# A second Strassen level for three of the seven products of the first GEMM, in a kernel of retention and a two-layer network

## The chip, the cores and the metric

The kernel runs on one core of one Trainium2 chip. The metric is the time of one execution on the device, in microseconds (us); lower is better. A core has a matrix engine (TensorE, PE in the profile), a vector engine (VectorE, DVE), a scalar engine (ScalarE, ACT), a general engine (GpSimd, POOL), and a queue that issues most transfers (SyncE, SP). Each runs its own instructions in the order in which they were written, and waits on semaphores where it needs another's result.

## The reference

A retention layer feeds a two-layer network. 4 batches, 8 heads, 768 steps, head size 64; the result is seen as 3072 tokens of 512 features; the network has 2048 hidden features. All is float32.

```python
for t in range(S):
    state = gamma[None, :, None, None] * state + np.einsum('bhd,bhe->bhde', k[:, :, t], v[:, :, t])
    y[:, :, t] = scale * np.einsum('bhd,bhde->bhe', q[:, :, t], state)
x = np.ascontiguousarray(attn_out.transpose(0, 2, 1, 3)).reshape(B * S, H * D)
h = x @ w_in
g = np.where(h > 0.0, h, alpha * (np.exp(np.minimum(h, 0.0)) - 1.0))
return (g @ w_out).astype(np.float32)
```

## The kernel before, in words

The tokens are cut into six blocks of 512, counted from 1 here (tb 0 to 5 in the code). For each block the kernel runs GEMM 1 (hidden = input times w_in), the ELU, and GEMM 2 (output = hidden times w_out). Data lie transposed: features on partitions, tokens along the free dimension. The retention of the next block (scores, states, outputs; L257 to L350) is put between pieces of GEMM 2, and writes the next block's input into xb.

Block 1 is multiplied plainly. From block 2 on, both GEMMs use the Winograd form of Strassen's algorithm (strassen, L455): each matrix is cut into four quarters, and seven products of quarters, summed up in a certain way, take the place of eight. Products 1, 6 and 5 are added up in one PSUM bank (pa) one after the other, with a copy to SBUF by ScalarE after each (kept, L447), products 7 and 4 in a second (pd), product 2 in a third (pb). VectorE adds a bank and a kept copy (plus, L452). The left factors are sums of weight quarters, made once (combine_w_in for w_in, combine_w_out for w_out); the right factors are differences of quarters of the input (combine_x into xt for GEMM 1).

GEMM 1 is run in four parts n, one for each four of the sixteen tiles of 128 hidden rows: two tiles of the upper half and the two of the lower half that belong to them. A part with its four results C11, C12, C21, C22 (two row tiles by 256 tokens each) is called a quadruple here. Each product of a part is four matmuls of 128x128 weights and 256 columns (L497), so one of the seven products takes 16 matmuls in a block. Each result goes through the ELU (elu, L370): relu and exp on ScalarE into a tile r, and later one operation on VectorE that puts max(h, exp - 1) into the hidden tiles gC11 to gC22. That last operation is kept in a list, later, and written into VectorE's order when the next ELU starts. When a part's C12 is done, two differences are made, T3 = C22 - C12 and T1 = C12 - C11 (L509), T1 in the place of C12.

GEMM 2 of block 2 has one level (second), with combine_w_out beside it, which also stores second-level weights to scratch2. From block 3 on GEMM 2 has two levels (second_twice): each of its seven products is itself made of seven, of four matmuls with 128 columns each (L618). The right factors of a product are four differences (inputs, L607) into a tile ts, of which there are two; the weights come from DRAM, 256 KB each, through a ring of 11 tiles (fetch_small): each use of a tile is followed by the fetch of the one 11 further on, in the order of the list USE. The ring lies in memory that the pools stage and t4 used before, and opens when GEMM 2 of block 2 is over.

The order on each engine is that of the program text, since it asks for a manual schedule. The main loop (L784) lets the parts of GEMM 1 overlap: it starts products 1 and 2 of a part before products 3 and 4 of the part before (the generator tail), and does the same between GEMM 1 and GEMM 2 and between blocks. The next block's q, k and v are loaded on SP in GEMM 1 (load), and v is scaled on GpSimd as it lands (scale_v, L239).

## Time and profile before

The median of 8 runs is 663.36 us (661.96 to 665.23). The profile is of one execution.

| | before |
|---|---|
| profiled execution | 665.23 us |
| its span, first to last instruction | 663.2 us |
| mean granted TensorE clock | 0.994 |
| TensorE busy | 641.1 us (97%) |
| VectorE busy | 434.8 us (66%) |
| ScalarE busy | 228.9 us (35%) |
| GpSimd busy | 24.4 us (4%) |
| blocks 3, 4, 5, 6 start on TensorE at | 252.58, 354.31, 457.55, 563.14 us |
| moved by DMA | 123.64 MB, 186 GB/s |

Busy time is the time in which an engine has an instruction at work, a weight load (PEld) being counted apart. A group in the profile is all instructions of one source line, engine and operation; what stands behind "idle before" is how long the engine stood before them and what ended it. The chain is found from the last instruction backwards. "issue" is time in which an engine waited for nothing that the profile shows.

### The profile page before, as it was taken

What the parts mean: (1) busy time and instruction counts of PE and PEld (TensorE: products, weight loads), DVE (VectorE), ACT (ScalarE), POOL (GpSimd) and SP (SyncE); (2) the same over time, 40 slices, a digit from 0 to 9 for tenths busy, and PEclk for the clock granted to TensorE, in tenths of its full rate; (3) what the DMA queues carried; (4) which work ended last, traced back from release to release, by engine and by line L of the source; (5) the groups of instructions that cost most, each with busy time, mean ns of one, the idle gap of its engine ahead of it and who ended that gap; (6) DMA issues with size and microseconds to landing.
All of it is one profiled execution on the core that took longest, in us unless ns stands there. A gap on an engine that the chain in (4) does not pass through costs nothing.

```text
span 663.2 us, 14662 instructions
## 1 busy us (share of the span) xinstructions
PE 641.1 (97%) x6144; PEld 540.8 (82%) x6144; DVE 434.8 (66%) x769; ACT 228.9 (35%) x432; POOL 24.4 (4%) x28
## 2 busy tenths in 40 slices
PE   4899999999999999999999999999999899999997
PEld 4764455458888888889999889899889899888996
DVE  5698678566757744549765557767357948355974
ACT  7477542014541002543112553112455111455211
POOL 1000100001100000200000200000200000000000
PEclk9899999999999999999999999999999989999999
DMA  9648977549115758505777604677702758300793
GB/s 341 233 145 302 333 232 234 144 134 374 71 64 167 249 207 278 230 1 189 218 217 235 240 1 123 213 229 247 289 0 62 246 165 266 109 1 16 220 305 128
DMA packets 63825, 123.64 MB, mean 186 GB/s; under 512 B 5136, under 2 KB 22544, under 8 KB 61712
## 3 DMA queue, kind: packets, MB, share of 16 engines
q1 hardware_dynamic: 63760, 122.70, 55.7%
q8 instruction: 49, 0.80, 0.5%
q14 instruction: 16, 0.13, 0.1%
HBM read 100.66 MB, written 22.02 MB: 185 GB/s over the span
## 4 chain that ended last, share of the span: by engine, by line
PE 95%; DVE 2%; DMA 1%; issue 1%; SPq 0%; ACT 0%; DVEq 0%
PE pa L497 21%; PE pa L618 15%; PE pd L497 10%; PE pd L618 7%; PE hp L396 6%; PE pb L497 5%; PE pa L410 4%; PE pa L555 4%; PE pb L618 4%; PE pd L555 2%; PE kv L287 2%; PE y L335 2%; PE pd L410 2%; PE pb L410 2%; PE y L311 2%; PE sc L265 2%
## 5 line engine op out<-in xcount | busy, mean ns | idle before, releaser
L452 DVE TENSOR_TENSOR h<-pd,m 128x512 f32<-128x512 f32 x42 | 29.1, 692 | 86.5 <-ACT m L447 69.5
L447 ACT COPY m<-pa 128x512 f32<-128x512 f32 x63 | 36.4, 578 | 109.6 <-PE pa L497 73.7
L626 ACT COPY ms<-pa 128x128 f32<-128x128 f32 x84 | 22.4, 266 | 127.6 <-PE pa L618 124.5
L374 ACT ACTIVATE r<-r 128x512 f32<-128x512 f32 x96 | 60.7, 632 | 3.0
L618 PE MATMUL pd<-ts,wq 128*128 128x128 f32 x448 | 59.9, 277 | 0.3 <-DVE res L630 0.3
L618 PE MATMUL pa<-ts,wq 128*128 128x128 f32 x448 | 59.2, 275 | 0.0
L373 ACT ACTIVATE r<-h 128x512 f32<-128x512 f32 x60 | 38.0, 632 | 57.1 <-DVE h L452 57.1
L618 PEld LDWEIGHTS pd<-ts,wq 128*128 128x128 f32 x448 | 54.5, 192 | 1.2 <-DVE res L630 0.9
L618 PEld LDWEIGHTS pa<-ts,wq 128*128 128x128 f32 x448 | 54.8, 192 | 0.2
L618 PE MATMUL pa<-gC,wq 128*128 128x128 f32 x384 | 52.1, 278 | 0.4 <-ACT ms L626 0.4
L376 DVE SCALAR_TENSOR_TENSOR gC<-r,h 128x512 f32<-128x512 f32 x60 | 42.0, 700 | 11.4 <-ACT r L374 11.4
L618 PEld LDWEIGHTS pa<-gC,wq 128*128 128x128 f32 x384 | 47.3, 192 | 1.7 <-ACT ms L626 0.5
L239 POOL TENSOR_TENSOR kvn<-kvn,vf 128x512 f32<-128x512 f32 x20 | 22.4, 1119 | 456.1 <-DMA kvn<-in_qkv_dram 397.0
L497 PE MATMUL pa<-xb,w_s 128*128 128x256 f32 x160 | 37.8, 379 | 0.0
L497 PE MATMUL pa<-xb,w_a 128*128 128x256 f32 x160 | 37.8, 379 | 0.0
L497 PE MATMUL pa<-xt,w_s 128*128 128x256 f32 x160 | 37.8, 379 | 0.0
L497 PE MATMUL pa<-xt,w_b 128*128 128x256 f32 x160 | 37.8, 379 | 0.0
L497 PE MATMUL pd<-xt,w_b 128*128 128x256 f32 x160 | 37.8, 379 | 0.0
L497 PE MATMUL pb<-xb,w_a 128*128 128x256 f32 x160 | 37.8, 379 | 0.0
L497 PE MATMUL pd<-xt,w_s 128*128 128x256 f32 x160 | 37.8, 379 | 0.0
L630 DVE TENSOR_TENSOR res<-pd,ms 128x128 f32<-128x128 f32 x56 | 16.1, 288 | 29.1 <-PE pd L618 26.7
L497 PEld LDWEIGHTS pa<-xt,w_b 128*128 128x128 f32 x160 | 30.4, 190 | 4.1
(121 smaller groups left out, 1100.6 us busy)
## 6 DMA issues: line engine op xcount, KB each, us to landing
wq<-scratch_dram SPq DMA_DIRECT2D x196, 256.0 KB, 4.0
wraw<-in_w_dram SPq DMA_DIRECT2D x16, 1024.0 KB, 6.0
qk<-in_qkv_dram SPq DMA_DIRECT2D x24, 512.0 KB, 8.7
kvn<-in_qkv_dram SPq DMA_DIRECT2D x24, 512.0 KB, 9.3
scratch_dram<-so SPq DMA_DIRECT2D x22, 512.0 KB, 3.3
ws<-scratch_dram SPq DMA_DIRECT2D x7, 1024.0 KB, 7.1
scratch_dram<-w_s SPq DMA_DIRECT2D x8, 512.0 KB, 7.4
out_dram<-res SPq DMA_DIRECT2D x12, 256.0 KB, 3.3
```

Source lines behind the costliest of these rows:

```text
L239: eng.tensor_tensor(out=kv[:, 1], in0=kv[:, 1], in1=vf[:, i].unsqueeze(2).to_broadcast([C, H, D]), op=ALU.mult)
L373: nc.scalar.activation(r, h, AF.Relu, scale=-1.0)
L374: nc.scalar.activation(r, r, AF.Exp, scale=-1.0)
L376: later.append(lambda: nc.vector.scalar_tensor_tensor(g, r, -1.0, h, ALU.add, ALU.max))
L396: nc.tensor.matmul(hp, lhsT=w[n][:, fi, j // 2, j % 2, :], rhs=xb[:, j, :], start=(j == 0), stop=(j == 3))
L410: nc.tensor.matmul(ops[d], lhsT=wo[:, row, d * P : (d + 1) * P], rhs=g_plain[row * NF + f], start=(f == 0 and row == 0), stop=(f == NF - 1 ...
L447: nc.scalar.copy(m, ps)
L452: nc.vector.tensor_tensor(out=h, in0=ps, in1=m, op=ALU.add)
L497: nc.tensor.matmul(ps[:, fi, :], lhsT=w[:, fi, j2, :], rhs=x[:, j2, :], start=(begin and fi == 0 and j2 == 0), stop=(j2 == 1), skip_group_ ...
L555: nc.tensor.matmul(ps[:, d, :], lhsT=ws[:, 2 * d + f // 4, f % 4, :], rhs=gq[INPUT2[j]][:, f, :], start=(begin and f == 0 and d == 0), sto ...
L618: nc.tensor.matmul(ps, lhsT=w[:, f, :], rhs=ts[j][k][:, f, :], start=(begin and f == 0), stop=(f == 3), skip_group_check=True,)
L626: nc.scalar.copy(m, ps)
```

## The change

From the third block on (tb 2 to 5), three of GEMM 1's seven products, M2, M3 and M7, are each made by seven smaller ones (first_twice), over all 2048 hidden rows at once: four matmuls of 128 columns for each. Their second-level weights (four of seven; the rest are quarters of the weights as they are) are summed up on GpSimd in block 2 (combine_small), stored to a new scratch3, and fetched through the same ring, which now opens with the last product of block 2's GEMM 2 (change); their right factors are made by combine_x_twice. The finished M2, M3, M7 are put into gC11, gC12 and gC22, where the hidden values will be.

After that the quadruples are worked one by one: M1, M6 and M5 are added up in a bank of their own (first_rest into qa), M4 in pd, and five sums on VectorE end in the results (first_end and sixth): C11 = M1 + M2, u2 = M1 + M6 + M7, C22 = M1 + M6 + M5 + M7, C12 = M1 + M6 + M5 + M3, C21 = u2 + M4. ScalarE makes no copies here. elu gets a depth: the last operation of an ELU is put behind up to two later ones, and r has three tiles. T3 is made behind C12's ELU; T1 is now made in GEMM 2, as C22 - C11 after C11 has become T3 + C11 (later_t1). The loads of the next block are issued between the products of first_twice, its scalings written between the quadruples. combine_x runs at the start of a block. In block 2, combine_w_in runs two steps at a time and earlier, and the first fetches of w_out come after GEMM 1. GEMM 2 and the retention are the same matmuls as before.

```diff
-    w_a = [const.tile([P, 2, 2, 2, P], FP32, name=f"w_a{n}") for n in range(NQ)]
-    w_b = [const.tile([P, 2, 2, 2, P], FP32, name=f"w_b{n}") for n in range(NQ)]
-    w_s = [const.tile([P, 3, 2, 2, P], FP32, name=f"w_s{n}") for n in range(NQ)]
+    w_a_, w_b_ = (const.tile([P, NQ, 2, 2, 2, P], FP32, name=x) for x in ("w_a", "w_b"))
+    w_s_ = const.tile([P, NQ, 3, 2, 2, P], FP32, name="w_s")
+    w_a, w_b, w_s = ([x[:, n] for n in range(NQ)] for x in (w_a_, w_b_, w_s_))
...
-    def elu(g, h):
-        r = epool.tile([P, 512], FP32, name="r", tag="r")
-        nc.scalar.activation(r, h, AF.Relu, scale=-1.0)
-        nc.scalar.activation(r, r, AF.Exp, scale=-1.0)
-        flush()
-        later.append(lambda: nc.vector.scalar_tensor_tensor(g, r, -1.0, h, ALU.add, ALU.max))
+    def elu(g, h, depth=1, then=None):
+        r = epool.tile([P, 512], FP32, name="r", tag="r", bufs=3)
+        e = r if len(h.shape) == 2 else r.rearrange("p (a c) -> p a c", c=P)
+        nc.scalar.activation(e, h, AF.Relu, scale=-1.0)
+        nc.scalar.activation(e, e, AF.Exp, scale=-1.0)
+        def last():
+            nc.vector.scalar_tensor_tensor(g, e, -1.0, h, ALU.add, ALU.max)
+            if then:
+                then()
+        while len(later) >= depth:
+            later.pop(0)()
+        later.append(last)
...
+            if j == 4:
+                behind_last()
...
+    TWICE = [2, 3, 7]
+    SMALL = {5: 0, 6: 1, 7: 2, 3: 3}
+    small_w, to_fetch, before = [], [], []
+    for tb in range(2, NTB):
+        for j in TWICE:
+            m1, m2, *mine = [(tb, 0, j, k) for k in (1, 2, 6, 7, 5, 4, 3)]
+            to_fetch += [m1] + before[:1] + [m2] + mine[:2] + before[1:] + mine[2:3]
+            before = mine[3:]
+        to_fetch, before = to_fetch + before, []
+        for j in ORDER2:
+            mine = [(tb, 1, j, k) for k in (1, 2, 6, 7, 5, 3, 4)]
+            to_fetch += mine[:2] + before + mine[2:5]
+            before = mine[5:]
+        to_fetch, before = to_fetch + before, []
+    to_fetch = [x for x in to_fetch if x[1] == 1 or x[3] in SMALL]
     def fetch_small():
         if not to_fetch:
             return
-        tb, j, k = to_fetch.pop(0)
+        name = to_fetch.pop(0)
+        _, which, j, k = name
         t = ring.tile([P, 4, P], FP32, name="wq", tag="wq")
-        if k in (1, 2, 4):
+        if k in SMALL:
+            n = SMALL[k]
+            nc.sync.dma_start(
+                t.rearrange("p f d -> p (f d)"), (scratch3, scratch2)[which][j - 1, :, 512 * n : 512 * n + 512]
+            )
+        else:
             q = 4 * SLOT[j] + {1: 0, 2: 1, 4: 3}[k]
             nc.sync.dma_start(t.rearrange("p f d -> p (f d)"), scratch[q])
+        small_w.append((name, t))
+    W_IN = {2: w_a_[:, :, :, 1], 7: w_s_[:, :, 1], 3: w_s_[:, :, 2]}
+    def combine_small(j):
+        t = stage.tile([P, 4, 4, P], FP32, name="wi", tag="stage")
+        a11, a12, a21, a22 = (W_IN[j][:, 2 * r : 2 * r + 2, :, c, :] for r in range(2) for c in range(2))
+        s1, s2, s3, s4 = (t[:, k].rearrange("p (n f) c -> p n f c", f=2) for k in range(4))
+        tt = lambda o, x, y, op: nc.gpsimd.tensor_tensor(out=o, in0=x, in1=y, op=op)
+        tt(s1, a21, a22, ALU.add)
+        tt(s2, s1, a11, ALU.subtract)
+        tt(s3, a11, a21, ALU.subtract)
+        tt(s4, a12, s2, ALU.subtract)
+        nc.sync.dma_start(scratch3[j - 1], t.rearrange("p k f d -> p (k f d)"))
+    xs = {}
+    def quarters_of_input(t, b11, b12, b21, b22):
+        sub = lambda o, x, y: nc.vector.tensor_tensor(out=o, in0=x, in1=y, op=ALU.subtract)
+        sub(t[:, 0], b12, b11)
+        yield
+        sub(t[:, 1], b22, t[:, 0])
+        yield
+        sub(t[:, 2], b22, b12)
+        yield
+        sub(t[:, 3], b21, t[:, 1])
+    def combine_x_twice(part):
+        if part == 0:
+            xs[0] = tpool.tile([P, 4, 4, P], FP32, name="ts", tag="ts")
+            b = [xb[:, 2 + k].rearrange("p (h t c) -> p t h c", h=2, t=2)[:, u] for k in range(2) for u in range(2)]
+            names, at = (2, 3), slice(0, 2)
         else:
...
+            b = [xt_[:, 2:3, k, P * u : P * u + P] for k in range(2) for u in range(2)]
+            names, at = (7,), slice(2, 3)
+        t = xs[0][:, :, at]
+        for _ in quarters_of_input(t, *b):
+            pass
+        for n, j in enumerate(names):
+            b11, b12, b21, b22 = (x[:, n] for x in b)
+            xs[j] = {1: b11, 2: b21, 3: b22, 4: t[:, 3, n], 5: t[:, 0, n], 6: t[:, 1, n], 7: t[:, 2, n]}
+    PLACE = {2: "C11", 3: "C12", 7: "C22"}
+    def first_twice(tb, j):
+        dst = PLACE[j]
+        place = lambda name, r, t: gq[name][:, 4 * r : 4 * r + 4, P * t : P * t + P]
+        full = lambda t: t.rearrange("p a (b c) -> p (a b) c", c=P)
+        def product(k, ps, begin):
+            if k in SMALL:
+                name, w = small_w.pop(0)
+                assert name == (tb, 0, j, k)
+                lhs = [w[:, f, :] for f in range(4)]
+            else:
+                r, c = {1: (0, 0), 2: (0, 1), 4: (1, 1)}[k]
+                lhs = [W_IN[j][:, 2 * r + f // 2, f % 2, c, :] for f in range(4)]
+            for f in range(4):
+                nc.tensor.matmul(
+                    ps[:, f, :], lhsT=lhs[f], rhs=xs[j][k], start=(begin and f == 0), stop=True,
+                    skip_group_check=True,
+                )
+            if k in SMALL:
+                fetch_small()
+        def lift(ps, o=None):
+            if o is None:
+                o = full(mpool.tile([P, 2, TH], FP32, name="m", tag="m"))
+            nc.scalar.copy(o, ps)
+            return o
+        def plus(r, t, ps, m):
+            nc.vector.tensor_tensor(out=place(dst, r, t), in0=ps, in1=m, op=ALU.add)
+        pa = full(bank("a"))
+        product(1, pa, True)
+        m1 = lift(pa)
+        yield
+        pb = full(bank("b"))
+        product(2, pb, True)
+        plus(0, 0, pb, m1)
+        product(6, pa, False)
+        u2 = lift(pa)
+        pd = full(bank("d"))
+        product(7, pd, True)
+        m7 = lift(pd)
+        yield
+        product(5, pa, False)
+        plus(1, 1, pa, m7)
+        yield
+        product(4, pd, False)
+        plus(1, 0, pd, u2)
+        yield
+        product(3, pa, False)
+        lift(pa, place(dst, 0, 1))
+    def first_rest(n, j, ps):
+        w, x = {
+            1: (w_a[n][:, :, 0], xb[:, 0:2, half[0]]), 6: (w_s[n][:, 0], xt[1]), 5: (w_b[n][:, :, 0], xt[0]),
+            4: (w_b[n][:, :, 1], xt[3]),
+        }[j]
+        for fi in range(2):
+            for j2 in range(2):
+                nc.tensor.matmul(
+                    ps[:, fi, :], lhsT=w[:, fi, j2, :], rhs=x[:, j2, :],
+                    start=(j in (1, 4) and fi == 0 and j2 == 0), stop=(j2 == 1), skip_group_check=True,
+                )
+    def first_end(n, name, ps, x=None):
+        g = gq[name][:, 2 * n : 2 * n + 2, :]
+        nc.vector.tensor_tensor(out=g, in0=ps, in1=g if x is None else x, op=ALU.add)
+        g = g.rearrange("p a b -> p (a b)")
+        def combine():
+            mine = lambda x: gq[x][:, 2 * n : 2 * n + 2, :].rearrange("p a b -> p (a b)")
+            nc.vector.tensor_tensor(out=mine("T3"), in0=mine("C22"), in1=mine("C12"), op=ALU.subtract)
+        return lambda: elu(g, g, 2, combine if name == "C12" else None)
+    def later_t1(ns):
+        for n in ns:
+            mine = lambda x: gq[x][:, 2 * n : 2 * n + 2, :].rearrange("p a b -> p (a b)")
+            nc.vector.tensor_tensor(out=mine("T1"), in0=mine("C22"), in1=mine("C11"), op=ALU.subtract)
...
             if j == 2:
+                flush()
                 next_input(2)
             if j == 5:
                 next_input(6)
...
+                if j == 6:
+                    later_t1((0, 1))
                 next(cur)
+                if j == 6:
+                    later_t1((2, 3))
...
-    for j in ORDER2[:3]:
-        fetch(1, j)
+    ring = tpool = None
...
+    sides = itertools.chain(combine_w_in(1), combine_w_in(2)), combine_w_in(3), iter(()), iter(())
+    smalls = [2], [], [7], [3]
+    for n in range(NQ):
+        load(2 * CPB + n)
+        cur = first(n)
+        for at in range(3):
+            next(cur)
+        for _ in tail:
+            pass
+        for s in cur:
+            next(sides[n], None)
+            next(sides[n], None)
+            if s == "gap":
+                break
+        for _ in sides[n]:
+            pass
+        tail = cur
+        for j in smalls[n]:
+            combine_small(j)
+    for j in ORDER2[:3]:
+        fetch(1, j)
+    for m in range(2 * CPB, 3 * CPB):
+        scale_v(m)
+    def change():
+        nonlocal ring, tpool
+        early.close()
+        ring = ctx.enter_context(tc.tile_pool(name="ring", bufs=RING))
+        tpool = ctx.enter_context(tc.tile_pool(name="tpool", bufs=2))
+        for _ in range(RING):
+            fetch_small()
+        combine_x_twice(0)
+    cur = second(1, change)
+    next(cur)
+    next(cur)
+    for _ in tail:
+        pass
+    flush()
+    for step, s in enumerate(cur):
+        retention_step(2, step)
+    tail = iter(())
+    for tb in range(2, NTB):
         more = tb + 1 < NTB
...
+        qa = []
+        def rest(n, j):
+            if j == 1:
+                qa.append(ps_r.tile([P, 2, TH], FP32, name="qa", tag="r"))
+            first_rest(n, j, qa[n])
+        rest(0, 1)
+        for _ in tail:
+            pass
+        combine_x()
+        combine_x_twice(1)
+        rest(1, 1)
+        tail = iter(())
+        for at, j in enumerate(TWICE):
+            cur = first_twice(tb, j)
             next(cur)
+            next(tail, None)
             next(cur)
             for _ in tail:
                 pass
...
+            if at == 2:
+                first_end(1, "C11", qa[1])()
             next(cur)
...
+            if at == 1:
+                first_end(0, "C11", qa[0])()
             tail = cur
+            if more:
+                load((tb + 1) * CPB + at)
+        next(tail)
+        next(tail, None)
+        if more:
+            load((tb + 1) * CPB + 3)
+        u2 = {}
+        def sixth(n):
+            rest(n, 6)
+            u2[n] = mpool.tile([P, 2, TH], FP32, name="m", tag="m")
+            nc.vector.tensor_tensor(out=u2[n], in0=qa[n], in1=gq["C22"][:, 2 * n : 2 * n + 2, :], op=ALU.add)
+        def fourth(n):
+            pd = bank("d")
+            first_rest(n, 4, pd)
+            return first_end(n, "C21", pd, u2[n])
+        sixth(0)
+        for n in range(NQ):
+            if n < 2:
+                rest(n + 2, 1)
+                first_end(n + 2, "C11", qa[n + 2])()
+            elif n == 2:
+                fourth(1)()
+            else:
+                fourth(2)()
+            rest(n, 5)
+            ends = [first_end(n, name, qa[n]) for name in ("C22", "C12")]
+            ends[0]()
+            if n < 3:
+                ends[1]()
+            if n == 0:
+                fourth(0)()
+            if n < 3:
+                sixth(n + 1)
+            if n == 1:
+                sec = second_twice(tb, (lambda: combine_x_twice(0)) if more else lambda: None)
+            if more:
+                scale_v((tb + 1) * CPB + n)
+            if n in (1, 2):
+                next(sec)
+        next(sec)
+        ends[1]()
+        end = fourth(3)
+        next(sec)
+        end()
+        flush()
+        for step, s in enumerate(sec):
+            if step > 0:
+                retention_step(tb + 1, step - 1)
+            if s == ORDER2[-1]:
+                break
+        tail = sec
```

## The prediction

> **What bounds the kernel now.** I read the page's busy table and its chain first, then the groups, the waits of TensorE, and at last the timeline of one block, engine by engine.
>
> ```profile
> PE 641.1 (97%) x6144; PEld 540.8 (82%) x6144; DVE 434.8 (66%) x769; ACT 228.9 (35%) x432; POOL 24.4 (4%) x28
> ...
> PE 95%; DVE 2%; DMA 1%; issue 1%; SPq 0%; ACT 0%; DVEq 0%
> ```
>
> TensorE is busy for 97% of the span and is 95% of the chain. VectorE has a third of its time free, on average over stages. The waits of TensorE from 252 us on name little:
>
> ```profile
> PE kv L287 <- issue: 2.2, 1, 2.2
> PE sc L265 <- issue: 2.1, 2, 1.3
> PE y L311 <- issue: 0.5, 1, 0.5
> PE pa L618 <- ACT ms L626: 0.4, 1, 0.4
> PE pd L618 <- DVE res L630: 0.3, 2, 0.2
> ```
>
> So nearly every wait for another engine is hidden, and each matmul removed is worth its pitch, until one of these waits comes out. TensorE's timeline gives the pitches (start, duration, group; the record counts a float32 matmul twice):
>
> ```profile
> 357.76 1.05 PE L618 MATMUL pa<-gC,wq 128*128 128x128 f32 x8
> 358.65 1.06 PE L618 MATMUL pd<-ts,wq 128*128 128x128 f32 x8
> 359.55 1.89 PE L497 MATMUL pa<-xt,w_s 128*128 128x256 f32 x8
> 361.28 1.89 PE L497 MATMUL pd<-xt,w_s 128*128 128x256 f32 x8
> 363.00 1.89 PE L497 MATMUL pa<-xt,w_b 128*128 128x256 f32 x8
> ```
>
> Starts are 1.727 us apart for four matmuls of 256 columns, 0.893 us for four of 128. Durations overlap and are no price. VectorE's timeline, in the same way:
>
> ```profile
> 365.55 0.69 DVE L452 TENSOR_TENSOR h<-pd,m 128x512 f32<-128x512 f32 x1 [4.63 <-ACT m L447]
> 366.16 0.68 DVE L376 SCALAR_TENSOR_TENSOR gC<-r,h 128x512 f32<-128x512 f32 x1
> ...
> 370.49 1.08 DVE L376 SCALAR_TENSOR_TENSOR gC<-r,h 128x512 f32<-128x512 f32 x1 [0.76 <-ACT r L374]
> 371.84 0.69 DVE L452 TENSOR_TENSOR h<-pd,m 128x512 f32<-128x512 f32 x1 [0.26 <-PE pd L497]
> 372.44 0.68 DVE L376 SCALAR_TENSOR_TENSOR gC<-r,pa 128x512 f32<-128x512 f32 x1
> 373.16 1.20 DVE L509 TENSOR_TENSOR gT<-gC,gC 128x512 f32<-128x512 f32 x1
> ```
>
> A 512-column operation takes 0.69 us, the next follows 0.61 us after its start, or 0.72 us if it reads the result (372.44 to 373.16). VectorE starts 0.20 us after TensorE's next group (371.84 after 371.64), ScalarE likewise. The two long ones, 1.08 and 1.20, lie beside GpSimd's operations, which began at 369.99 and 372.77 and take 1.04 us.
>
> **What the Trainium skill says.** "VectorE: DVE Perf Modes", section on the TRN2 errata, gives (N+151)/0.96 ns for a float32 tensor_tensor: 691 ns for 512. The trace has 692. "SBUF — State Buffer", section "Who interferes with whom": a DVE instruction with two SBUF inputs contends with a GpSimd one that reads SBUF, one with a single SBUF input doesn't. The trace agrees: both long operations read two SBUF tiles, and the PSUM sum at 371.84 is not longer. "TensorE: Matmul & The Clock Gate", section "Back-to-back issue gap": spacing is not proportional to columns, short matmuls pay more per column. Here 0.893 against half of 1.727, which is 0.864.
>
> **The change part by part.** I number the GEMM's seven Winograd products M1 to M7 and the seven inside one of them p1 to p7; blocks count from 1, so blocks 3 to 6 change.
>
> *TensorE.* M2, M3 and M7 took 16 matmuls of 256 columns each, 4 x 1.727 = 6.91 us. They become 28 of 128 columns, 7 x 0.893 = 6.25 us. That saves 0.66 us a product, 1.96 a block, 7.8 us in four blocks. M1, M4, M5, M6 keep 64 matmuls in the block in another order; GEMM 2 and the retention keep theirs.
>
> *VectorE.* A quadruple (two row tiles of the hidden layer) had three sums from PSUM, four ELU ends, two differences: 9 operations. It now has five sums, four ends, T3, and T1 later: 11. The three split products add nine sums a block, their inputs eight short operations. That is 8 + 9 long ones (10.4 us) and about 2.5 us, on some 66 us busy in a block of 102 us: still below TensorE's total. What decides is where they lie; I laid the listed orders of the three engines beside each other with the prices above. Four places don't close.
>
> (1) Before p6 of M7. p6 adds on the bank of p1, so it waits for ScalarE's copy m1, which is queued behind the ELU of C11 of quadruple 0, whose VectorE sum is queued behind M3's sum after p5. From the start of M3's p5: 0.89 + 0.20, the sum ahead 0.61, the C11 sum 0.72, relu 0.67, exp 0.54 to the next (pitches 366.27, 366.94, 367.48 on ScalarE), copy 0.58, 0.04 to TensorE: 4.25 us. TensorE has four groups of 0.893 in between, 3.57 us. It stands 0.68 us, and 0.1 us more for the restart (after the wait at 657.06 the next group came 0.1 us late).
>
> (2) In the quadruples. From the end of M1 of quadruple 3 to u2 of quadruple 3, VectorE has 18 operations in order, C11 to u2, two or three of them dependent: 18 x 0.61 + 3 x 0.12 = 11.3 us, and 0.12 to the consumer. The M5 of quadruple 3 waits for that u2; TensorE has seven groups from the start of that M1, 12.09 us, less 1.93 until VectorE can start: 10.16 us. Shortfall 1.26 us, with restart 1.35.
>
> (3) Next, p7 of GEMM 2's first product wants bank d, freed by the C21 sum of quadruple 3: ten operations, a short one and the last latency, 7.15 us, against 6.86 us: 0.3 us.
>
> (4) After the states of the retention. Four T1 differences, 2.44 us, now stand ahead of the seven state updates (0.48 us apart at 323.16). From the end of GEMM 2's p4 of product 2 to p4's sum of product 6: 0.29 + 5 x 0.61 + 0.16 + 2.44 + 0.21 + 7 x 0.46 + 0.60, about 10.0 us with latencies, against eight groups and the states, 8 x 0.893 + 2.15 = 9.3 us. TensorE's p7 of product 7 waits 0.7, with restart 0.8. Block 6 has no retention.
>
> GpSimd's four scalings a block move: the loads are issued about 10, 16, 22 and 25 us into the block on SP, behind small-weight fetches that wait for TensorE, and land 9 us later; two scalings then fall into the quadruples. Each lengthens an ELU end, T3 or input difference by 0.4 to 0.5 us, or nothing beside a PSUM sum. I take 0.5 in all, ends 0 and 1.5.
>
> Sum for blocks 3 to 5: 0.8 + 1.35 + 0.3 + 0.8 + 0.5 = 3.75, less 1.96: +1.8 each, 5.4 us. Block 6: 0.8 + 1.35 + 0.3 - 1.96 = +0.5.
>
> *Block 2.* combine_w_in comes two at a time, eight operations of 0.61 to 0.72 in quadruple 0, beside nine others in 12.1 us: VectorE has the time, but a sum may come late. GpSimd gets 12 operations[...] for the small weights; they lie under TensorE and cost only by slowing VectorE. Three stores of 1 MB and the ws loads behind them on SP: an estimate from the trace: the last combined weights are there at about 170 us, eight GpSimd operations take 9 us, a store 3.3 us, so the last is stored at 182; the first ws lands 7.1 us after its issue and is wanted at 191.5. I take 0.5 us, ends 0 and 3.
>
> *DMA.* 48 more fetches of 256 KB, landing in 4.0 us. The ring of 11 is issued 11 products ahead, 9.8 us at 0.893. In block 3 the first can't start before M4 of GEMM 2 frees its staging tile (252.58), and p6 of M2 comes 2 x 1.727 + 2 x 0.893 = 5.2 us later; 0.4 + 4.0 fits by 0.8. Zero taken, up to 4 us once. Renamed weight tiles, the third r buffer and the T1 formula cost nothing of their own: no engine issues more for them. The tail is as before.
>
> *Total.* The waits put down to "issue", 4.9 us, lie in retention bursts; some may vanish where TensorE has stood shortly before. I take 0.6 off. 5.4 + 0.5 + 0.5 - 0.6 = +5.8 us on the profiled execution, span 663.2, execution 665.23. That one is the slowest of the eight shown; I add the change to the median, 663.36: **669.2 us**. Under 0.2% (1.3 us) a measurement of this kernel can't tell from no change.
>
> **Rivals.** *VectorE keeps up*, the other side: all four places close and the matmuls' 7.8 us come off: 655.5. For it: VectorE's total is below TensorE's. Against it: the quadruples need 18 operations in 10.16 us, 0.56 us each, and no row is that fast. It gets faster as soon as the new waits are below 1.96 us a block. *Even*: half of the waits are real, and they stand in for the "issue" waits: 8 of new waits against 7.8: 663.5. *Worse*: GpSimd's scalings fall where VectorE is late (1.0 more in three blocks), block 3's ring is late by 3, block 2 gives up 2: 669.2 + 8 = 677. *The matmuls don't get shorter*, as 128-column ones with weights from w_a were not seen: their weight loads are 128x128 in both rows, so I hold this below 2 in 100; it adds to Worse.
>
> **How the numbers follow.** Forecast (666 to 673): 0.61. Worse (673 to 678): 0.15. Even (662 to 665): 0.12. Faster (654 to 661.5): 0.12. Leaving out the lower tail and half of Worse gives 661 to 675. Faster 0.13, the same 0.10, slower 0.77.
>
> **What would show it.** Right: TensorE's page row near 6432 instructions, the busy total of VectorE some 45 us up; TensorE's waits name ScalarE's m copy four times at 0.7, u2 on VectorE at 1 us or more, res and gC21 sums. Wrong: VectorE idle in the quadruples with waits for TensorE, or no wait of TensorE above 0.3 us; waits for wq would be a transfer I held hidden. The prediction fails on the fast side if VectorE's pitch falls with operands in other banks, on the slow side if the backlog of the quadruples reaches the second stage uncut.

## The result and the profile after

The changed kernel takes 669.15 us in the median of 12 runs (666.42 to 670.66), against 663.4 us for the kernel before, measured beside it (33 runs): ratio 1.0078, 95% interval 1.0059 to 1.0097. It is slower by 3.9 to 6.4 us. The forecast was 669.2 us. Run once more beside other runs of the kernel before, it gave 668.35 against 664.14 us, ratio 1.0059 (1.0040 to 1.0077); so the change costs some 4 to 6 us.

The profiled execution has a span of 670.3 us (before 663.2) at a mean clock of 0.995. The page of after, busy table and chain:

```profile
PE 638.0 (95%) x6432; PEld 542.3 (81%) x6432; DVE 491.6 (73%) x869; ACT 230.2 (34%) x432; POOL 43.5 (6%) x40
...
PE 82%; DVE 12%; issue 3%; ACT 2%; DMA 1%; SPq 0%; DVEq 0%
```

TensorE's share of the chain fell from 95% to 82% and VectorE's rose from 2% to 12%: TensorE now stands waiting for sums. 6432 matmul records were announced, and VectorE's busy time is up by 56.8 us (45 announced). TensorE's waits in the same profile (what was waited for, us in total, times, longest):

```profile
PE y L315 <- issue: 3.7, 2, 2.7
PE qa L734 <- DVE m L1040: 3.2, 4, 0.8
...
PE pa L688 <- ACT m L698: 2.1, 4, 0.5
PE sc L269 <- issue: 1.8, 1, 1.8
PE y L339 <- issue: 1.3, 1, 1.3
PE kv L291 <- issue: 1.2, 1, 1.2
PE pd L777 <- DVE res L789: 0.8, 3, 0.5
...
PE pd L510 <- DVE h L465: 0.6, 1, 0.6
```

Two waits stand in each of the four changed blocks, which the kernel before did not have: for m, the copy of p1 of M7 by ScalarE (place 1), and for u2 of quadruple 3 (place 2, m in qa's row). The wait for h is in block 2. TensorE's timeline of block 4 in after shows both:

```profile
375.83 1.06 PE L688 MATMUL pb<-xt,w_s 128*128 128x128 f32 x8
377.41 1.16 PE L688 MATMUL pa<-ts,wq 128*128 128x128 f32 x8 [0.53 <-ACT m L698]
378.41 1.06 PE L688 MATMUL pd<-ts,wq 128*128 128x128 f32 x8
...
391.73 1.89 PE L734 MATMUL qa<-xb,w_a 128*128 128x256 f32 x8
393.67 1.99 PE L734 MATMUL qa<-xt,w_b 128*128 128x256 f32 x8
395.50 1.89 PE L734 MATMUL qa<-xt,w_s 128*128 128x256 f32 x8
...
402.41 1.89 PE L734 MATMUL pd<-xt,w_b 128*128 128x256 f32 x8
405.10 1.99 PE L734 MATMUL qa<-xt,w_b 128*128 128x256 f32 x8 [0.80 <-DVE m L1040]
406.93 1.05 PE L777 MATMUL pa<-gC,wq 128*128 128x128 f32 x8
```

Read the starts, not the numbers in brackets. From p2 to p6 of M7 it is 1.58 us in place of 0.893, and the next one comes 1.00 us later: 0.69 + 0.11 = 0.80 us lost. Before M5 of quadruple 3 (405.10) it is 2.69 us in place of 1.727, and 1.83 behind it: 0.96 + 0.10. M5 of quadruple 1 (393.67) has a smaller one that the list of waits leaves out: 1.94 and 1.83, 0.21 + 0.10.

Two differences between the two profiles are not the change's. Block 1 is the same program in both, and block 2 begins 2.2 us later in after (the twelve profiles below spread over that much), with a lower granted clock in one slice of block 1 (0.7, before 0.8). And the bursts of 64x64 matmuls of the retention, whose waits are put down to "issue", took 32.6 us in blocks 3 to 5, against 30.7 before; in the second profile of the changed kernel they took 30.0.

### The profile page after: what moved, and what is told of

Read it like the earlier page. It is cut to its first block, busy times and chain, and to the rows that moved or that the text cites. A ratio compares the mean times of both kernels' runs of the same rounds, so it can differ in the third digit from the quotient of the medians.

```text
span 670.3 us, 15507 instructions
## 1 busy us (share of the span) xinstructions
PE 638.0 (95%) x6432; PEld 542.3 (81%) x6432; DVE 491.6 (73%) x869; ACT 230.2 (34%) x432; POOL 43.5 (6%) x40
## 4 chain that ended last, share of the span: by engine, by line
PE 82%; DVE 12%; issue 3%; ACT 2%; DMA 1%; SPq 0%; DVEq 0%
PE pa L777 14%; PE qa L734 8%; PE pd L777 7%; PE pa L688 6%; PE hp L409 6%; PE pa L423 4%; PE pa L568 4%; PE pb L777 3%; PE pa L510 3%; PE pd L688 3%; DVE gC L383 3%; DVE gC L742 2%; PE pd L568 2%; PE pd L423 2%; PE pb L423 2%
## 5 line engine op out<-in xcount | busy, mean ns | idle before, releaser
L379 ACT ACTIVATE r<-gC 128x512 f32<-128x512 f32 x64 | 40.4, 631 | 48.6 <-DVE gC L742 47.8
L383 DVE SCALAR_TENSOR_TENSOR gC<-r,gC 128x512 f32<-128x512 f32 x64 | 44.8, 716 | 0.0
L742 DVE TENSOR_TENSOR gC<-qa,gC 128x512 f32<-128x512 f32 x48 | 31.6, 686 | 7.3 <-PE qa L734 7.1
L734 PE MATMUL qa<-xt,w_b 128*128 128x256 f32 x128 | 31.1, 386 | 3.4 <-DVE m L1040 3.2
L645 DVE TENSOR_TENSOR ts<-gC,ts 128x512 f32<-128x512 f32 x48 | 33.0, 689 | 0.8
L645 DVE TENSOR_TENSOR ts<-gC 128x512 f32<-128x512 f32 x48 | 32.9, 684 | 0.0
L734 PEld LDWEIGHTS qa<-xt,w_b 128*128 128x128 f32 x128 | 23.5, 190 | 9.6 <-DVE m L1040 6.5
L423 PE MATMUL pa<-gC,w_s 128*128 128x512 f32 x64 | 30.6, 600 | 0.0
L734 PE MATMUL qa<-xt,w_s 128*128 128x256 f32 x128 | 30.2, 379 | 0.0
L734 PE MATMUL qa<-xb,w_a 128*128 128x256 f32 x128 | 30.1, 379 | 0.0
```

The lines of the kernel that those rows point to most:

```text
L379: nc.scalar.activation(e, h, AF.Relu, scale=-1.0)
L383: nc.vector.scalar_tensor_tensor(g, e, -1.0, h, ALU.add, ALU.max)
L423: nc.tensor.matmul(ops[d], lhsT=wo[:, row, d * P : (d + 1) * P], rhs=g_plain[row * NF + f], start=(f == 0 and row == 0), stop=(f == NF - 1 ...
L645: sub = lambda o, x, y: nc.vector.tensor_tensor(out=o, in0=x, in1=y, op=ALU.subtract)
L734: nc.tensor.matmul(ps[:, fi, :], lhsT=w[:, fi, j2, :], rhs=x[:, j2, :], start=(j in (1, 4) and fi == 0 and j2 == 0), stop=(j2 == 1), skip_ ...
L742: nc.vector.tensor_tensor(out=g, in0=ps, in1=g if x is None else x, op=ALU.add)
```

## The experiments

To compare profiles I took stretches of TensorE's timeline by start times, which leaves out these two. A is the time from the first inner product of M2 to the first M6 of the quadruples (21 groups of 0.893 us, 18.75 at full pitch); in block 4 of after it is 363.18 to 383.10. B goes from there to the first group of GEMM 2 (13 groups of 1.727, 22.45). C is GEMM 2 from its first group to the next block's first M1 (in block 6 to the start of the last matmul), less each retention burst up to the group behind it. In the kernel before, GEMM 1 from the block's start to GEMM 2's first group took 46.68 us in blocks 4 and 5, and one more M4 group (1.73) lay in GEMM 2; so 48.41 answers to 5.24 + A + B (5.24 us from the block's start to M2's first inner product in blocks 4 to 6; in block 3 no group of an earlier GEMM 2 lies in between, and both figures are 1.79 us smaller). C is 182.06 us in four blocks. Three profiles have a stretch of seven groups that ran at a granted clock of 0.5 to 0.7 and took 8.06 to 8.07 us in place of 6.45: before (block 5), late T3 and small sums cut (both block 3); C is corrected for it. The sum is 4 x (5.24 + A + B - 48.41) + (C - 182.06) + 0.91 for block 2, which is told below (small sums cut does without the 0.91).

| kernel | A, mean | B, mean | C, four blocks | sum against before | measured, medians | ratio (95%) |
|---|---|---|---|---|---|---|
| changed | 19.91 | 23.81 | 183.40 | +4.5 | +5.8 | 1.0078 (1.0059 to 1.0097) |
| changed, again | 19.91 | 23.87 | 183.12 | +4.4 | +4.2 | 1.0059 (1.0040 to 1.0077) |
| late ELU | 19.12 | 23.96 | 183.10 | +1.6 | +1.4 | 1.0026 (1.0006 to 1.0045) |
| late inputs | 19.91 | 23.44 | 188.30 | +7.9 | +8.6 | 1.0142 (1.0090 to 1.0193) |
| no scaling | 19.91 | 23.72 | 183.73 | +4.4 | +3.1 | 1.0048 (1.0031 to 1.0065) |
| no ELU | 19.12 | 22.45 | 182.82 | -4.7 | -3.5 | 0.9948 (0.9931 to 0.9965) |
| late T1 | 19.91 | 23.79 | 184.60 | +5.6 | +5.9 | 1.0082 (1.0051 to 1.0112) |
| late T3 | 19.91 | 23.03 | 187.59 | +5.5 | +5.4 | 1.0064 (1.0039 to 1.0089) |
| late sums, all | 19.12 | 22.94 | 184.38 | -1.2 | -0.7 | 0.9990 (0.9965 to 1.0015) |
| small sums cut | 19.91 | 23.99 | 182.94 | +3.8 | +4.6 | 1.0064 (1.0041 to 1.0086) |
| moved sums | 19.12 | 23.25 | 182.66 | -1.7 | -1.4 | 0.9980 (0.9960 to 0.9999) |

The sums agree with the medians within 1.4 us, so these stretches hold most of the effect. Each sum is of one profile, and some hold what another execution may not have: an "issue" wait outside of a burst (late T1, 1.2 us), or a quadruple late by a scaling. The misses of 1.2 to 1.3 us (changed, no scaling, no ELU) are not explained.

**Late ELU.** The ELU of C11 of quadruple 0 is begun later:

```diff
             next(cur)
             next(tail, None)
+            if at == 2:
+                first_end(0, "C11", qa[0])()
             next(cur)
             for _ in tail:
...
                 first_end(1, "C11", qa[1])()
             next(cur)
-            if at == 1:
-                first_end(0, "C11", qa[0])()
```

> Edit: the C11 sum and ELU of quadruple 0 are written behind the copy m1 of M7 and M3's p4, not ahead of them. Theory (p6 of M7 waits 0.69 us a block for m1, queued behind that ELU): the wait of L688 for m is gone in the trace and the time falls by 4 x 0.69, about 2.8 us, to 666.4. Rival (VectorE's backlog sets the pace of the whole first GEMM, so time won ahead of the quadruples is lost again at the M5 products): the wait for u2 grows by as much and the time stays at 669.

Measured: 665.51 us against 664.16. No wait of TensorE for m is left, and A falls from 19.91 to 19.12 us in all four blocks, 0.79 each, 3.2 us together; against the kernel before, the median fell by 2.9 to 4.4 us (from +4.2 or +5.8 to +1.4). In block 4, p2 and p6 of M7 now follow each other at full pitch:

```profile
374.30 1.06 PE L688 MATMUL pb<-xt,w_s 128*128 128x128 f32 x8
375.19 1.06 PE L688 MATMUL pa<-ts,wq 128*128 128x128 f32 x8
```

Place 1 is shown, in its cause and its size. The wait for u2 stayed (four times 0.80), and a fifth came, in block 3, beside a scaling.

**Late inputs.** Half of the input differences of GEMM 2's first product stand ahead of u2 of quadruple 3; they are moved back by one quadruple, to ask whether u2 is late because of these two operations or because VectorE is behind as a whole.

```diff
-            if n in (1, 2):
+            if n in (2, 3):
                 next(sec)
```

> Edit: the four input differences of GEMM 2's first product come one quadruple later on VectorE, two of them behind u2 of quadruple 3. Simple count (only the 18 operations ahead of that u2 matter): 16 operations, 1.22 us less, so the M5 wait of 0.97 us goes in four blocks and the time falls by 3.9 us to 665.3. Backlog theory (VectorE owes about as many operations until the last C21 sum, wherever they stand): the M5 wait shrinks, TensorE's p7 of GEMM 2's first product waits for bank d instead, by 1 us or more, and the time is 669 to 673, not lower.

Measured: 672.8 us against 664.16. TensorE's waits in this profile:

```profile
PE pd L777 <- DVE gC L742: 5.0, 4, 1.3
...
PE pa L688 <- ACT m L698: 2.1, 4, 0.5
PE qa L734 <- DVE m L1040: 1.8, 4, 0.5
```

The wait for u2 fell by 1.4 us in all, and a new one of 5.0 us for the C21 sum of quadruple 3 came at p7 of GEMM 2's first product. That is place 3, which had almost closed: from u2 to this sum VectorE works without a gap, so the two operations put there meet the next consumer. Ahead of u2 it has gaps now, and the wait still fell by only 0.35 us a block where two operations, 1.22 us, had left. VectorE in block 4, at the first sum behind M5 of quadruple 2:

```profile
399.79 1.29 DVE L742 TENSOR_TENSOR gC<-qa,gC 128x512 f32<-128x512 f32 x2 [0.63 <-PE qa L734]
```

It stood 0.63 us for that M5, and from there C22, C12, two ELU ends, T3 of quadruple 1 and u2 itself (402.92) come without a gap. So VectorE is not behind as a whole: with 16 operations in place of 18, what holds u2 is this shorter row, six operations from one M5 to the next.

**No scaling.** The scalings by GpSimd for blocks 4 to 6 are left out.

```diff
-            if more:
-                scale_v((tb + 1) * CPB + n)
```

> Leaves out GpSimd's scaling of v for blocks 4 to 6, so these blocks' retention is computed from unscaled values. Theory: contention with VectorE costs about 0.5 us in each of three blocks, 667.6. Rival (GpSimd's contention is what makes VectorE late in the quadruples): the wait for u2 goes in blocks 3 to 5 and the time falls by 3 us or more, to 666 or below. If a PSUM sum or an idle stretch takes the scalings: 669.

Measured: 667.24 us against 664.16. The waits for u2 are unchanged (four times 0.8), so the scalings don't make them. B is 23.72 us in each block. With the scalings and the same wait for u2 it lay between 23.72 and 24.57: they cost 0.16 us or less in most blocks, and 0.6 to 0.85 us in one block of some profiles (block 3 of the late ELU, block 5 of the second profile of the changed kernel). Set against the kernel before, the median fell by 1.1 to 2.7 us; the stretches explain less than that, and why is left open. So the 667.6 us expected was met, but not shown to be met for the reason given.

**No ELU.** The ELU in blocks 3 to 6 is left out, with its work on ScalarE and VectorE.

```diff
-        return lambda: elu(g, g, 2, combine if name == "C12" else None)
+        return lambda: combine() if name == "C12" else None
```

> Leaves out the ELU (relu, exp and VectorE's end) of the first GEMM in blocks 3 to 6; sums and T3 stay. Theory (matmuls became 7.8 us shorter, all the rest is TensorE waiting for VectorE and ScalarE): the waits at L688 and L734, 2.5 us a block, go, and the time is 669.15 - 10 - 1, about 658. Rival (the small matmuls or their weight fetches don't bring 7.8 us): the waits go, and the time stays above 661.5.

Measured: 660.62 us against 664.16, not the 658 expected. Now B is at full pitch, 22.45 us, and every wait of TensorE for m and for u2 is gone. GEMM 1 is then 1.60 us shorter per block than before, 6.4 in four; at pure pitch it would be 1.97. The matmul saving is real, and 0.37 us of it goes to small gaps inside A. Of the 7.8 us, 1.5 go there in four blocks, 0.9 in block 2, and 0.9 in GEMM 2 of block 5 (C 45.69 us, before 44.83), which leaves 4.5; the medians show 3.5.

**Late T1.** All four T1 differences are moved from product 6 to product 7 of GEMM 2.

```diff
+            if j == 7:
+                later_t1(range(4))
             if at + 1 < 7:
                 inputs(ORDER2[at + 1])
...
-                if j == 6:
-                    later_t1((0, 1))
                 next(cur)
-                if j == 6:
-                    later_t1((2, 3))
```

> The changed kernel with one edit: the four T1 differences of GEMM 2 stand directly ahead of the inputs of product 5 (during product 7) and no longer around product 6. This tests place 4 of the prediction alone. The prediction's size, 0.7 + 0.1 us in each of blocks 3 to 5, would make the median 669.15 - 2.4 = 666.7 us. What the trace of the changed kernel shows, one wait of TensorE for res of 0.49 us in block 5 and nothing in blocks 3 and 4, would make it 669.15 - 0.6 = 668.5 us. Expected: 668.5 us, with the waits of TensorE for m (four times 0.5) and for u2 (four times 0.8) unchanged.

Measured: 669.86 us against 663.97, no gain where 668.5 was expected. The wait of 0.49 us in block 5 is gone, and one of 0.96 came in block 6, at p7 of product 5. TensorE's timeline there:

```profile
644.13 1.16 PE L777 MATMUL pd<-ts,wq 128*128 128x128 f32 x8 [0.96 <-DVE res L789]
```

Block 6 has no retention burst in which VectorE could catch up. Why block 5 alone had the wait in the changed kernel is in VectorE's timeline of after, block 4 first, then block 5:

```profile
432.58 1.29 DVE L755 TENSOR_TENSOR gC<-gC,gC 128x512 f32<-128x512 f32 x2
433.78 0.42 DVE L302 TENSOR_TENSOR xt<-kv,carry 128x256 f32<-128x256 f32 x1
434.24 1.67 DVE L302 TENSOR_TENSOR xt<-kv,xt 128x256 f32<-128x256 f32 x4
435.94 0.42 DVE L302 TENSOR_TENSOR carry<-kv,xt 128x256 f32<-128x256 f32 x1
...
537.78 1.29 DVE L755 TENSOR_TENSOR gC<-gC,gC 128x512 f32<-128x512 f32 x2
538.98 0.42 DVE L302 TENSOR_TENSOR xt<-kv,carry 128x256 f32<-128x256 f32 x1
539.51 2.79 DVE L302 TENSOR_TENSOR xt<-kv,xt 128x256 f32<-128x256 f32 x6
```

Behind the T1 differences come six state updates in block 4 and seven in block 5; 0.46 us more, and the wait stands. Block 3 has seven as well, but its states burst took 3.49 us where those of blocks 4 and 5 took 2.01, and VectorE caught up in it. In all eleven profiles of changed kernels that burst of block 3 is the long one (3.0 to 4.9 us). This is read from timelines; no run changed the updates alone.

**Late T3.** The four T3 differences go to GEMM 2, two behind product 2, two ahead of product 7's inputs (later_t3 holds the operation that combine held).

```diff
-        return lambda: elu(g, g, 2, combine if name == "C12" else None)
+        return lambda: elu(g, g, 2, None)
...
+            if j == 6:
+                later_t3((2, 3))
             if at + 1 < 7:
                 inputs(ORDER2[at + 1])
...
+            if j == 2:
+                later_t3((0, 1))
             before = cur
             yield j
```

> The changed kernel with one edit: the four T3 differences (0.69 us each on VectorE) leave the delayed ends of the ELU and come in GEMM 2 instead, two behind product 2 and two ahead of the inputs of product 7. Three of them stood in VectorE's queue ahead of the sum u2 of quadruple 3. This tests whether the wait of M5 of quadruple 3 (four times 0.80 + 0.1 us) is the length of VectorE's queue. Theory (too much work on VectorE in this stretch): the wait at M5 falls to nothing. If nothing else follows, the median is 669.15 - 3.6 = 665.5 us. Rival (the work is only moved): the T1 differences of product 6 follow directly behind, so that product 7 waits for VectorE's adding in 1 to 2 us in blocks 3 to 5, and the median is 667 to 670 us. Should the wait at M5 stay at 0.8, the queue was not its cause, and the median stays at 669.2 us. Expected: the rival, 668 us.

In this kernel and the next, the step that makes C11 + T3 (next_input(2)) stands ahead of the moved sums and reads an older T3, so products 6 and 4 of GEMM 2 work on other values; the instructions are the same in number and size. Measured: 669.33 us against 663.97. TensorE's waits for VectorE in blocks 4 to 6 of this profile, from the timeline (the two of 0.16 us left out):

```profile
438.36 1.16 PE L778 MATMUL pd<-ts,wq 128*128 128x128 f32 x8 [1.06 <-DVE res L790]
...
542.71 1.16 PE L778 MATMUL pd<-ts,wq 128*128 128x128 f32 x8 [1.53 <-DVE res L790]
...
640.02 1.16 PE L778 MATMUL pd<-ts,wq 128*128 128x128 f32 x8 [1.02 <-DVE res L790]
```

The wait for u2 is no longer listed, which shows place 2: it was the length of VectorE's queue. By the starts, 0.24 of 0.96 us are left in block 4:

```profile
402.68 1.89 PE L734 MATMUL pd<-xt,w_b 128*128 128x256 f32 x8
404.65 1.99 PE L734 MATMUL qa<-xt,w_b 128*128 128x256 f32 x8
```

B fell by 0.78 to 0.84 us a block against the two profiles of the changed kernel. And C rose by 4.2 to 4.5 us, because T3 and T1 now stood together ahead of product 7: the rival was right.

**Late sums, all.** The late ELU, the late T3 and the late T1 together: the edit is the three diffs above, one after the other.

```diff
+            if at == 2:
+                first_end(0, "C11", qa[0])()
...
+            if j == 7:
+                later_t1(range(4))
+            if j == 6:
+                later_t3((2, 3))
...
+            if j == 2:
+                later_t3((0, 1))
```

> The changed kernel with three edits of order together: the ELU of C11 of quadruple 0 begins behind ScalarE's copy of M7's first inner product, the T3 differences come behind product 2 and ahead of the inputs of product 7 of GEMM 2, and the T1 differences come ahead of the inputs of product 5. The same instructions, 6432 matmuls and 869 of VectorE. If the three waits of the changed kernel are what the matmul saving was lost to, TensorE waits neither for m, nor for u2, nor for res at product 7, and the median is 669.15 - 3.5 (the late ELU, as measured alone) - 3.6 (the wait for u2) - 0.6 (place 4) = 661.5 us, ahead of the kernel before (663.4 to 664.2). Rival: VectorE's queue is simply too long over the block, and the waits show up elsewhere in GEMM 2; then 664 to 666 us.

Measured: 663.29 us against 663.97, level with before. None of the listed waits for m and u2 is left. GEMM 1 is 1.1 us a block shorter than before, and C is 2.3 us longer, 1.3 of them in block 6 (the 0.96 us wait for res again). The expected 661.5 was 1.8 us too low.

**Small sums cut.** GpSimd's weight sums of block 2 are replaced by fills, so that it reads no SBUF there.

```diff
-        tt(s1, a21, a22, ALU.add)
-        tt(s2, s1, a11, ALU.subtract)
-        tt(s3, a11, a21, ALU.subtract)
-        tt(s4, a12, s2, ALU.subtract)
+        nc.gpsimd.memset(t.rearrange("p k f d -> p (k f d)"), 0.0)
```

> The changed kernel, with GpSimd's twelve weight sums of block 2 (four for each of M2, M3 and M7) replaced by three fills with zeros, which read nothing; the weights of those inner products are then zeros, so this part of the computation is left out. The transfers of these weights stay. Tests whether the 0.75 us by which block 2 is longer than before comes from VectorE and GpSimd reading SBUF at the same time. If so, TensorE's wait of 0.55 us for h in block 2 goes, and the median is 669.15 - 0.75 = 668.4 us. Rival: block 2 is late for another reason (the load of these sums' transfers, or the start); then that wait stays and the median is 669.2 us. Expected: 668.4 us.

The weights of these inner products are then zeros. Measured: 668.56 us against 663.97. The wait for h at L510 is gone. GEMM 1 of block 2, from its first group to the first of GEMM 2, takes 44.89 us before, 45.79 to 45.81 in every other kernel of the table, and 44.89 here. So the price of these sums is 0.91 us. It falls on the eight of them that run in block 2; four run in block 1 (116.94 to 122.53), and their price is not in this figure. The fills also ran earlier, all in block 1, so the edit takes GpSimd's sums out of this stretch altogether; that reading beside VectorE is what costs is in the timelines. In after, GpSimd and VectorE:

```profile
168.08 1.72 POOL L634 TENSOR_TENSOR wi<-w_s 128x512 f32<-128x512 f32 x1 [45.55 <-ACT m L460]
169.87 1.59 POOL L634 TENSOR_TENSOR wi<-wi,w_s 128x512 f32<-128x512 f32 x1
```

```profile
167.98 0.69 DVE L444 TENSOR_TENSOR w_b<-w_b 128x512 f32<-128x512 f32 x1
168.70 1.64 DVE L444 TENSOR_TENSOR w_s<-w_b,w_a 128x512 f32<-128x512 f32 x1
170.38 1.64 DVE L444 TENSOR_TENSOR w_s<-w_a,w_s 128x512 f32<-128x512 f32 x1
```

Without the sums the last two of these take 0.69 us each:

```profile
167.33 0.69 DVE L444 TENSOR_TENSOR w_s<-w_b,w_a 128x512 f32<-128x512 f32 x1
168.06 0.69 DVE L444 TENSOR_TENSOR w_s<-w_a,w_s 128x512 f32<-128x512 f32 x1
```

In after the engines take turns: VectorE's operation from 168.70 ends 0.54 us after GpSimd's end at 169.80, and GpSimd's from 169.87 ends 1.12 us after VectorE's end at 170.34. The Trainium skill, "SBUF — State Buffer", section "Who interferes with whom", says that VectorE with two SBUF inputs and GpSimd reading SBUF share a port as an exclusive lock; these lines agree, at 1.64 us for an operation of 0.69.

**Moved sums.** The late ELU; of the T3 differences only that of quadruple 1 is moved, to just ahead of the step that reads it; of the T1 differences two stay, two go to product 7.

```diff
+        return lambda: elu(g, g, 2, (lambda: t3(n)) if name == "C12" and n != 1 else None)
...
                 flush()
+                t3(1)
                 next_input(2)
...
+            if j == 7:
+                later_t1((2, 3))
             if at + 1 < 7:
                 inputs(ORDER2[at + 1])
...
-                if j == 6:
-                    later_t1((2, 3))
```

> The changed kernel with three edits of order, and all of the computation kept: the ELU of C11 of quadruple 0 begins behind ScalarE's copy of M7's first inner product; one of the four T3 differences, that of quadruple 1, comes in GEMM 2 directly ahead of the step that reads it; the T1 differences of quadruples 2 and 3 come ahead of the inputs of product 5, those of 0 and 1 stay at product 6. Theory (each place of VectorE's queue has about one difference of slack): no wait for m; the wait for u2 falls from four times 0.80 to 0.1 to 0.2 us; no wait of 0.96 us for res in block 6 such as all four moved T1 differences made; the wait of 0.49 us for res in block 5 goes. In the trace the stretch of the inner products is 19.1 us, that of the quadruples 23.0 to 23.2 (23.8 in the changed kernel), GEMM 2 of block 6 stays at 47.35 us. The median is 669.15 - 4 x 0.8 (ELU) - 4 x 0.7 (u2) - 0.5 = 662.6 us, ratio 0.998 to the kernel before. Rival: the moved sums make new waits in GEMM 2 as in the two kernels that moved them before; then the median is 664 us or more.

Measured: 662.79 us against 664.14, ratio 0.9980 (0.9960 to 0.9999), and 0.992 of the changed kernel measured beside it. All of the work is done. It is the fastest whole kernel here, ahead of before by 0.2%, about what can be told from no change. TensorE's waits in its profile:

```profile
PE pd L778 <- DVE res L790: 0.9, 2, 0.8
...
PE pd L510 <- DVE h L465: 0.6, 1, 0.6
PE qa L734 <- DVE m L1041: 0.6, 1, 0.6
```

The one wait for u2 that is left stands in block 3 beside a scaling; in blocks 4 to 6 B is 22.99 to 23.17 us. The wait for res in block 5 is gone (C there 44.89 in place of 45.74), and one of 0.8 came in block 6, whose C rose by 0.6; I had expected it to stay. It stands at p7 of product 6, where the changed kernel had 0.16 us:

```profile
622.47 1.16 PE L778 MATMUL pd<-ts,wq 128*128 128x128 f32 x8 [0.77 <-DVE res L790]
```

The 0.61 us more are one operation of VectorE, the moved T3 of quadruple 1, which stands ahead of this product's inputs. The two moved T1 differences made no wait in block 6, where all four had made one of 0.96.

**Changed, again.**

> The changed kernel itself, unaltered, so that the experiments have it on the same chip and beside the same runs of the kernel before. Expected: a ratio of 1.0078 as at first, 1.006 to 1.0095; the waits of TensorE for m (four times 0.52 us) and u2 (four times 0.80 us) the same to 0.05 us, while the issue waits in the bursts of 64x64 matmuls, 8.3 us in all in the first profile, differ: the other kernels showed 4.6 to 7.3 us.

Measured: 668.35 us against 664.14, ratio 1.0059, just below the range expected. The waits for m and u2 repeat to 0.05 us, with a fifth for u2, in block 5 (3.7 us in five). The issue waits were 5.1 us in place of 8.3.

## Why the prediction was right, point by point

The verdict and the time held, and the mechanism did: VectorE's and ScalarE's order in front of TensorE cost more than the matmuls saved. Within the sum of +5.8 some terms were too high and some too low. That the first median met the forecast within 0.1 us is partly luck: the second lies 0.8 lower, the stretches give +4.4 to +4.5, and errors of both signs cancel in the sum.

- **Matmul saving, 1.96 a block.** Right: 1.97 at pitch. But the inner products don't keep their pitch: A is 0.37 us a block longer even without the wait for m, 0.22 of it ahead of and behind p3 of M7 (1.01 and 1.00 us), the rest in three pitches of 0.94 us. This was not in the sum.
- **Place 1, 0.68 + 0.1.** 0.69 + 0.11, in four blocks; the late ELU took 0.79 away. Right.
- **Place 2, 1.25 + 0.1.** The count of 18 operations was right for this kernel: in block 3, C11 of quadruple 3 starts at 289.63 and u2 at 300.37, with 18 operations from the one to the end of the other, 11.4 us against 11.3 counted. The loss came in two parts, 1.06 us at M5 of quadruple 3 and 0.31 at M5 of quadruple 1: 1.37 us against 1.35. I had looked for it in one place, but the earlier stop lengthens TensorE's time by as much. The count is not the only limit: the late inputs left 16 operations, and u2 was still 0.45 us late behind M5 of quadruple 2.
- **Place 3, 0.3.** 0.1 us of wait (block 4): from u2's start at 404.36 to p7 at 411.43 it is 7.07 us in place of the 7.15 counted, and the stop at M5 makes TensorE's side 0.1 us longer. How near it was to a larger wait the late inputs showed (1.3 us).
- **Place 4, 0.8 in each of blocks 3 to 5.** The step that failed most: 0.49 us of wait in block 5, 0.85 in that block's C, and next to nothing in blocks 3 and 4. I took seven state updates for each block; block 4 has six, and a burst with an issue wait gives VectorE time. The three blocks cost about 1.1 us, not 2.4.
- **Scalings, 0.5 in each of blocks 3 to 5.** Too high on average: 0.16 or less in most blocks, 0.6 to 0.85 in one of some profiles. A single collision is dearer than the 0.4 to 0.5 that I took (0.9 us for two ends at 285.66: 2.17 us where two take 1.28), and rarer.
- **Block 2, 0.5.** 0.91, by the mechanism named, within the ends given. One reading behind it was not shown by the line named: beside the PSUM sum at 371.84 no GpSimd operation ran (one had ended at 371.03, the next began at 372.77). In after, the PSUM sum at 171.94 lies within GpSimd's operation from 171.43 to 173.15 and takes 0.68 us, so the reading itself holds.
- **Issue waits, -0.6.** Not to be seen: 4.0 to 8.3 us in the profiles of changed kernels, 4.9 before. Their places are not random: in all eleven profiles one stands in block 3's states burst and one in the y bursts (L315) of blocks 4 and 5 each, in five also one in block 4's scores; in before they stand in block 3's scores and y bursts, block 4's scores and block 5's states. The sizes differ from execution to execution (0.4 to 2.7 us), and what sets places and sizes stays open.
- **DMA.** No wait for wq in any profile of the table. Right.

So 5.4 + 0.5 for blocks 3 to 6 turns into 3.5 by the stretches: GEMM 1 +2.2 to +2.4, GEMM 2 +1.1 to +1.3. Together with block 2 that is +4.4.

The rival "VectorE keeps up" fell for the reason given against it. The kernels with late and with moved sums, though, show how much the order decided: with the same instructions in number and size GEMM 1 gains 1.1 and 0.8 us a block over before, and the whole is level with before. None of these orders brought the matmuls' 7.8 us.

## What to carry to other kernels

A cut of matmuls that adds sums is paid where the sums lie, not by VectorE's total: lay the engines' orders beside each other, count the operations between two consumers, and compare with TensorE's time between them. In a stretch where VectorE has no gap, moving an operation back helps only as far as the next consumer has slack: here two T1 differences found it at product 7 and four did not, and in block 6 a single T3 difference cost its whole 0.61 us at product 6. Spread them, and check the block that has no burst in which to recover. Once the queue is shorter, look for the row that starts at TensorE's last result, as the late inputs showed. Begin work that nobody waits for soon (an ELU) behind a copy that TensorE waits for.

## What the runs showed of the hardware that I had not expected

- A stop of TensorE is paid beyond the wait: the group behind it comes about 0.10 us late again (1.83 in place of 1.727, 1.00 in place of 0.893). From block 2 on, the twelve profiles have 172 stops of 0.15 us or more between two groups at full clock, and this follows 164 of them. It does not follow the three gaps of 0.05 us inside A (in block 4 of after, starts 364.97, 365.91 and 366.80 show the first of them).
- VectorE and GpSimd with SBUF inputs on both sides run one after the other: 512-column operations that take 0.69 us alone took up to 1.64 on VectorE, and GpSimd's sums took 1.27 to 1.72. Eight such sums cost 0.91 us of the kernel.
- The same prologue put block 2's start between 146.6 and 148.9 us in twelve profiles, and the "issue" waits in bursts of 64x64 matmuls ranged over 4 us. A single profile's span therefore says little on a change of 1%, while a stretch without these repeats: A is 19.91 us in every profile that had the wait, B of block 6 23.71 or 23.72 in every profile with the order of the changed kernel's quadruples and its ELU.
